# A convolution and a channel mix on one core: the start of the first pair in steps of 256 tokens, with its x loads on both sides of K's weights

## The chip, the core and the metric

One core of a Trainium2 chip runs the whole program in one launch. PE (TensorE) multiplies, ACT (ScalarE) and DVE (VectorE) work on tiles in SBUF and PSUM, POOL (GpSimd) and SP (SyncE) mostly issue DMAs. The metric is the device time of one execution in microseconds; the figure that counts is the median over runs. A profile is one execution recorded by the hardware.

## The reference

x is 8 x 4160 x 192 in float32. A causal convolution of 7 taps, one softmax-normalised set of taps for each of 8 heads of 24 channels, makes y. Then a channel mix with the token before:

```python
y  = causal_conv7(x, softmax(weight))            # per head
xk = mu_k * y + (1 - mu_k) * y_prev
xr = mu_r * y + (1 - mu_r) * y_prev
k  = maximum(xk @ w_k, 0)                        # 192 -> 1024
v  = (k * k) @ w_v                               # 1024 -> 192
out = sigmoid(xr @ w_r) * v
```

## The kernel before

The 8 sequences are worked on as 4 pairs; the two sequences of a pair lie in the two halves of the 128 partitions (64 channels of each), in three column blocks `c` of 64 channels. A pair is cut into **steps** of 512 tokens. The first pair has a first step of 256 and a last one of 256 (`sizes`, L62). K of a step is cut into **slots**: a slot is one PSUM tile of 1024 columns, two sequences of 512, that holds 128 rows of K for 512 tokens or 256 rows for 256 tokens, so a step of 256 has 4 slots and one of 512 has 8. Four slots make a **bundle**. `slots[2:8]` is put into another order (L73) so that bundle 0 needs only the first 512 columns of `w_k`.

For a slot, `k_mm` (L521) issues the matmuls into PSUM, `k_relu` (L545) is the ReLU on ACT, `k_square` (L551) squares on DVE. V's matmuls (`v_rows`, L615) follow some bundles later, R's (`r`, L586) in between. Before K, DVE makes `d = y - y_prev` (`diff`, L476), then `xk` and `xr` from it with a scale for each column block and one add (`scale` L505, `add_y` L515; `mix` calls both).

The convolution goes by **groups** of blocks of x (L88 to L98). For the first pair the groups 0, 1 and 2 (3, 4 and 4 blocks of 120 tokens) are convolved straight into the transposed layout by `conv_t` (L361), in which x is the stationary operand, and copied from PSUM to `yT` by `to_yT`. Group 3 goes through `conv_mm` (64x128 tiles of the array) and transposes on PE, groups from 4 on through `conv_tiles` (64x64 tiles), a buffer in DRAM and a transposing DMA (`y_write`, `y_read`).

The program is recorded in a fixed order: each engine's queue is the order in which the functions are called. `prologue` (L756) issues the loads and makes the masks and the band matrix `toe`. `bundle_first`, `bundle_second` and `bundle_third` are written out by hand; tables (`mix_a`, `mix_b`, `mix_c`, `late`) hold DVE work that is put into a bundle at given places, `rest` bundles follow one pattern. All loads of x and of the weights go through POOL's queue, in the order of the calls: x of group 1, first half of `w_k` (two DMAs, one for each half of the partitions), x of group 2, second half of `w_k`, x of group 3, `w_r`, `w_v`, x of group 4. The DMAs share eight semaphores in turn, so the ninth waits for the first to land. x of group 0 comes through the queues of ACT and SP.

PSUM is a ring of four tiles of two banks. A write into one bank of a tile waits for the reads of earlier data of this tile, of its other bank too, where the program has such a wait.

Of the kernel before, what the change touches and what calls it, by code (L numbers as in the profile page):

```python
# [14 lines left out]
def kernel(  # L15
# [43 lines left out]
    slots = []  # L59
    first_step = {}  # L60
    for p in range(NPAIR):
        sizes = [STEP // 2] + [STEP] * (S // STEP - 1) + [STEP // 2] if p == 0 else [STEP] * (S // STEP)  # L62
        t0 = 0
        first_step[p] = len(steps)
        if p == NPAIR - 1:
            sizes.append(NPAIR * TAIL)
        for L in sizes:
            ns = L * NF // STEP
            steps.append((p, t0, L, len(slots), ns))
            slots += [(len(steps) - 1, j) for j in range(ns)]  # L70
            t0 += L
    T0, LAST = S - TAIL, len(steps) - 1
    slots[2:8] = slots[4:8] + slots[2:4]  # L73
    NSLOT = len(slots)


# [21 lines left out]
        assert S <= base <= NROW  # L98


    xbs = {}

    def x_tile(g):
        p, base, nb, _, on_pe = groups[g]
        xb = three.tile([P, GB, 2, D], BF16, tag="xb", name="xb")
        xbs[g] = xb
        if g > 4:

            nc.vector.memset(xb[0:1, 0, 0, 0:2], 0.0)  # L109
        if base == 0:  # L110
            nc.gpsimd.memset(xb[0:32, 0, :, :], 0.0)  # L111
        if not on_pe and base + 2 * nb * HB > S:
            n0 = nb - (base + 2 * nb * HB - S) // HB - 1
            nc.gpsimd.memset(xb[Q:P, n0:nb, :, :], 0.0)

    def load_x(g):
        p, base, nb, _, on_pe = groups[g]
# [105 lines left out]
    def softmax():  # L223
        nc.vector.tensor_reduce(out=w_max, in_=w_raw, axis=mybir.AxisListType.X, op=ALU.max, negate=True)
        nc.scalar.activation(out=w_exp, in_=w_raw, func=AF.Exp, bias=w_max, accum_out=w_sum)
        nc.scalar.preload_act_table(AF.Sigmoid)
        xbs[0] = three.tile([P, GB, 2, D], BF16, tag="xb", name="xb")
        for c in range(NC):
            cs = slice(c * Q, (c + 1) * Q)
            nc.scalar.copy(out=xbs[0][:, : groups[0][2], :, cs], in_=x_f32[:, :, :, cs])  # L230
        nc.vector.reciprocal(out=w_sum, in_=w_sum)
        nc.vector.tensor_scalar(
            out=w_nrm[0:H, 0:K], in0=w_exp, scalar1=w_sum, scalar2=None, op0=ALU.mult
        )
        nc.vector.transpose(out=w_tap, in_=w_nrm)
        for r in range(8):
            nc.tensor.matmul(
                out=w_per[:, :, r], lhsT=tap8[:, 8 - r : 8 - r + P], rhs=w_tap[0:8, 0:H], start=True, stop=True
            )
# [265 lines left out]
    def scale(s, i, *cs):  # L505
        L = steps[s][2]
        if s not in (xks, xrs)[i]:
            (xks, xrs)[i][s] = two.tile([P, NC, STEP], BF16, tag=("xk", "xr")[i], name=("xk", "xr")[i])
        t = (xks, xrs)[i][s]
        for c in cs:  # L510
            nc.vector.tensor_scalar(  # L511
                out=t[:, c, :L], in0=diffs[s][:, c, :L], scalar1=mu[:, i, c : c + 1], scalar2=None, op0=ALU.mult
            )
# [194 lines left out]
    for s, (p, t0, L, n0, ns) in enumerate(steps):  # L708
        fb = first_bundle[s]
        if s == 0:  # L710
            at(mix_a, 1, mix, s, 1)
            continue
        if s == 1:
            at(mix_b, 1, scale, s, 1, 0, 1)
            at(late, 2, scale, s, 1, 2)
            at(late, 2, add_y, s, 1)
        else:
            if s == 2:
                at(mix_c, 1, diff, s)
            elif s == 4:  # L720
                at(mix_b, fb - 1, diff, s)
            else:
                at(mix_c, fb - 2, diff, s)
            at(mix_b if s == 4 else mix_a, fb - 1, scale, s, 0, 0)
            at(mix_b, fb - 1, scale, s, 0, 1, 2)
            at(mix_c, fb - 1, add_y, s, 0)
            if s == 2:
                at(mix_a, fb, scale, s, 1, 0)
                at(mix_b, fb, scale, s, 1, 1)
            else:  # L730
                at(mix_c, fb - 1, scale, s, 1, 0)
                at(mix_a, fb, scale, s, 1, 1)
            at(mix_b, fb, scale, s, 1, 2)
            at(mix_b, fb, add_y, s, 1)
        if s == LAST - 1 or s < LAST and steps[s + 1][0] > p:
            at(late, fb - 1, keep_tail, p)
    for s, j, vb in quads:
        b = vb - (s == LAST)
        if 0 < s < LAST - 1:
            b = min(b, first_bundle[s + 2] - 2 + j)  # L740
        at(rq, b, r, s, j)
        at(rs, b, r_out, s, j)
        if s == LAST:
            at(late, vb, v_last, s, j)
        else:
            vq.setdefault(vb, []).append((s, j))
# [9 lines left out]
    def prologue():  # L756
        nc.sync.dma_start(
            out=w_raw,
            in_=weight,
        )  # L760
        nc.vector.memset(x_f32[0:32, 0, :, :], 0.0)
        nc.vector.memset(ones_t, 1.0)
        for st, eng in ((0, nc.scalar), (1, nc.sync)):
            load_x_first(eng, 0, P, 1, groups[0][2], st, st + 1)
        load_x_first(nc.scalar, 16, P, 0, 1, 0, 2)
        load_x_first(nc.sync, HALO, 16, 0, 1, 0, 2)
        load_mu(0, moe_mu_k)
        load_mu(1, moe_mu_r)
        nc.scalar.preload_act_table(AF.Exp)
        nc.vector.memset(zeros, 0.0)  # L770
        nc.vector.memset(w_nrm, 0.0)
        nc.vector.memset(ones6, 1.0)
        x_tile(1)
        load_x(1)
        masks_tap()
        select_equal(ident6, 2 * NC)
        masks_band()
        load_wk(0, DF // 2)

        for i in range(SHORT):  # L780
            q = slice(i % 4 * 32, i % 4 * 32 + 32)
            nc.tensor.matmul(
                out=warm_ps[q, 0, 0:1], lhsT=ones_t[:, 0:32], rhs=ones_t[:, 0:1], start=True, stop=True
            )
        warm(warm_ps, WARM[0])
        x_tile(2)
        softmax()
        warm(warm_ps, WARM[1])
        make_toe()
        load_x(2)  # L790
        load_wk(DF // 2, DF)
        select_equal(ident, P)
        x_tile(3)
        load_x(3)
        load_wr()
        load_wv()
        x_tile(4)
        load_x(4)

    def bundle_first(ns):  # L800
        new_yT(0)
        tiles = [ring.tile([P, 2, BANK], FP32, tag="k", name="ps_t") for _ in range(2)]
        for n, (g, c) in enumerate((g, c) for g in range(2) for c in range(NC)):
            o = tiles[n % 2][:, n // 2 % 2, :]
            conv_t(g, c, o, range(groups[g][2]))
            if n == 0:
                turn_mu()
            to_yT(g, c, o, 0, groups[g][2], nc.scalar.copy)
            if g == 0:
                diff(0, slice(c, c + 1))  # L810
                if c == 0:
                    nc.vector.tensor_copy(out=mu.rearrange("p i c -> p (i c)"), in_=warm_ps[:, 1, 0 : 2 * NC])
                mix(0, 0, slice(c, c + 1))

        diff(1, slice(0, 1))
        mix(1, 0, slice(0, 1))
        for n in ns[:2]:
            k_mm(n)
            k_relu(n)
        diff(1, slice(1, 3))  # L820
        scale(1, 0, 1, 2)
        add_y(1, 0, slice(1, 3))
        for n in ns[2:]:
            k_mm(n)
            k_relu(n)
        for n in ns:
            k_square(n)
        run(late, 0)

    def bundle_second(b, ns):  # L830

        act_, dve_ = nc.scalar.copy, nc.vector.tensor_copy
        g = 2
        k_mm(ns[0])
        k_relu(ns[0])
        k_mm(ns[1])
        tiles = [ring.tile([P, 2, BANK], FP32, tag="k", name="ps_t") for _ in range(2)]
        outs = [tiles[0][:, 0, :], tiles[1][:, 0, :], tiles[0][:, 1, :]]
        conv_t(g, 0, outs[0], range(4))
        to_yT(g, 0, outs[0], 0, 4, dve_)  # L840
        k_relu(ns[1])
        conv_t(g, 1, outs[1], range(4))
        to_yT(g, 1, outs[1], 0, 4, dve_)
        k_mm(ns[2])
        k_relu(ns[2])
        conv_t(g, 2, outs[2], range(4))
        to_yT(g, 2, outs[2], 0, 4, act_)
        k_mm(ns[3])
        k_square(ns[0])
        run(mix_a, b)  # L850
        conv_half(xt[b][0], 0)
        k_relu(ns[3])
        conv_half(xt[b][0], 1)
        k_square(ns[1])
        run(mix_b, b)
        conv_mm(*xt[b][1], 0)
        conv_mm(*xt[b][1], 1)
        run(mix_c, b)
        run(late, b)
# [133 lines left out]
```

## Time and profile before

| | us |
|---|---|
| median of 3 runs (lowest, highest) | 413.19 (413.01, 413.28) |
| span of the profiled execution | 412.2 |
| PE busy | 403.7 (98%) |
| DVE busy | 370.5 (90%) |
| ACT busy | 353.2 (86%) |
| POOL busy | 64.1 (16%) |

The span runs from the first to the last instruction of the program. The time of a run is 0.99 us longer than the span of the profiled execution. Busy time of an engine is the union of its instructions; matmuls are pipelined, and a single one is listed with its whole latency, so that a sum of durations is more than the busy time. Where a row of the timeline merges several instructions, its length is that of the whole group. Rows name tiles as out<-in. `ps_t` is PSUM of `conv_t`, `ps_k` of K, `ps_c` of the other convolutions, `ps_v` of V, `ps_r` of R; `k_sb` is K after the ReLU, `k` its square.

The total by part of the chain that ended last, as shares of the span:

```profile
PE 88%; DMA 4%; DVE 3%; ACT 2%; issue 1%; POOL 1%; SPq 0%; POOLq 0%
```

### The profile page before, as it was taken

To read this page: it belongs to the slowest core of one execution; us is meant where nothing else is said; L and a number is where in the kernel's file an instruction comes from. 1 tells how busy PE (TensorE), PEld (TensorE's weight loads), DVE (VectorE), ACT (ScalarE), POOL (GpSimd) and SP (SyncE) were. 2 spreads that over 40 slices of the span, in tenths; PEclk is the share of its full clock that TensorE was granted. 3 is DMA by queue.
4 is the path that set the end of the run, shared out by engine and by line. 5 is a ranking of instruction groups with operands and counts; after the bars stand their busy time and mean duration, and the time that the engine had idled before them with its cause. 6 is when DMAs were issued, how large, how long until landed. Compare 5 with 4: busy or idle time off the path is not lost.

```text
span 412.2 us, 16799 instructions
## 1 busy us (share of the span) xinstructions
PE 403.7 (98%) x7349; PEld 301.7 (73%) x7350; DVE 370.5 (90%) x672; ACT 353.2 (86%) x426; POOL 64.1 (16%) x100
## 2 busy tenths in 40 slices
PE   7899999999999999999999999999999999999996
PEld 5567767767867777776777777777777777777795
DVE  5999799999999998999999999999989898999973
ACT  6899978889988888988888899888889888787781
POOL 8622023022040201104040110304000000000000
PEclk9999999999999999999999999999999999999999
DMA  9999989959978894998769697897863926321223
GB/s 141 192 200 194 191 200 190 253 133 194 198 110 211 151 214 118 200 218 113 198 121 229 156 196 182 111 226 130 188 163 100 184 82 175 107 67 53 80 80 115
DMA packets 137241, 65.58 MB, mean 159 GB/s; under 512 B 87356, under 2 KB 137168, under 8 KB 137168
## 3 DMA queue, kind: packets, MB, share of 16 engines
q1 hardware_dynamic: 95840, 48.42, 44.9%
q0 software_dynamic: 40528, 15.53, 33.0%
q8 instruction: 57, 0.93, 0.9%
q10 hardware_dynamic: 800, 0.57, 0.4%
q14 instruction: 16, 0.13, 0.1%
HBM read 31.62 MB, written 37.09 MB: 167 GB/s over the span
## 4 chain that ended last, share of the span: by engine, by line
PE 88%; DMA 4%; DVE 3%; ACT 2%; issue 1%; POOL 1%; SPq 0%; POOLq 0%
PE ps_v L625 39%; PE ps_k L537 37%; PE ps_r L594 7%; PE ps_c L302 3%; DMA yT<-y_dram 2%; DMA wk<-in_moe_w_k_dram 2%; DVE k L563 1%; PE ps_v L577 1%; DMA y_dram<-y 1%; ACT k_sb L549 1%; ACT y L319 0%; DVE d L480 0%; POOL xb L136 0%; DVE xr L511 0%; SPq L424 0%
## 5 line engine op out<-in xcount | busy, mean ns | idle before, releaser
L549 ACT ACTIVATE k_sb<-ps_k 128x1024 bf16<-128x1024 f32 x260 | 253.1, 1037 | 36.1 <-PE ps_k L537 35.2
L563 DVE TENSOR_TENSOR k<-k_sb 128x1024 bf16<-128x1024 bf16 x260 | 172.6, 685 | 28.3 <-ACT k_sb L549 27.9
L537 PE MATMUL ps_k<-xk,wk 64*128 64x512 bf16 (+1 forms) x1632 | 191.0, 367 | 1.2 <-DMA wk<-in_moe_w_k_dram 0.7
L625 PE MATMUL ps_v<-wv,k 64*128 64x192 bf16 x4032 | 188.2, 243 | 0.2 <-DVE k L563 0.2
L625 PEld LDWEIGHTS <-k 64*128 64x128 bf16 x4032 | 167.7, 94 | 13.6 <-issue 4.0
L537 PEld LDWEIGHTS <-wk 64*128 64x128 bf16 x1632 | 79.9, 94 | 59.6 <-DMA wk<-in_moe_w_k_dram 0.9
L136 POOL DMA_DIRECT2D xb<-in_x_dram x62 | 45.1, 738 | 171.2 <-issue 81.8
L641 DVE TENSOR_TENSOR o_sb<-ps_v,r_sb 128x768 f32<-128x768 f32 x64 | 60.8, 951 | 2.6 <-issue 2.4
L605 ACT ACTIVATE r_sb<-ps_r 128x768 bf16<-128x768 f32 x65 | 53.3, 821 | 10.6 <-PE ps_v L625 9.9
L319 ACT CAST y<-ps_c 128x960 bf16<-128x960 f32 (+5 forms) x84 | 50.7, 685 | 0.0
L594 PEld LDWEIGHTS <-xr 64*128 64x128 bf16 x780 | 34.5, 94 | 15.2 <-issue 1.0
L594 PE MATMUL ps_r<-wr,xr 64*128 64x192 bf16 x780 | 43.1, 243 | 0.5 <-DVE o_sb L641 0.5
L511 DVE TENSOR_SCALAR xr<-d,mu 128x512 bf16<-128x512 bf16 (+1 forms) x102 | 35.1, 348 | 0.0
L480 DVE TENSOR_TENSOR d<-yT 128x1536 bf16<-128x1536 bf16 (+4 forms) x36 | 31.3, 870 | 2.0 <-ACT yT L381 1.1
L511 DVE TENSOR_SCALAR xk<-d,mu 128x512 bf16<-128x512 bf16 (+1 forms) x99 | 32.0, 352 | 0.1
L517 DVE TENSOR_TENSOR xr<-xr,yT 128x1536 bf16<-128x1536 bf16 (+1 forms) x33 | 31.0, 938 | 1.1
L517 DVE TENSOR_TENSOR xk<-xk,yT 128x1536 bf16<-128x1536 bf16 (+3 forms) x33 | 30.4, 921 | 0.1
L302 PEld LDWEIGHTS <-toe 64*64 64x64 bf16 x448 | 9.6, 106 | 11.7 <-issue 10.7
L302 PE MATMUL ps_c<-xb,toe 64*64 64x240 bf16 (+1 forms) x448 | 16.6, 265 | 0.2 <-ACT k_sb L549 0.2
L464 POOL COPY y_tail<-yT 128x195 bf16<-128x195 bf16 x4 | 3.2, 796 | 64.9 <-DMA yT<-y_dram 64.8
L111 POOL MEMSET xb<- 32x384 bf16 x3 | 1.2, 407 | 45.2 <-DVE xb L109 39.2
L371 PEld LDWEIGHTS <-xb 128*32 128x32 bf16 (+3 forms) x264 | 5.3, 119 | 1.9 <-ACT xb L230 1.1
(57 smaller groups left out, 63.0 us busy)
## 6 DMA issues: line engine op xcount, KB each, us to landing
out_dram<-o_sb SPq DMA_DIRECT2D x128, 192.0 KB
xb<-in_x_dram POOLq DMA_DIRECT2D x40, 240.0 KB, 8.2
y_dram<-y SPq DMA_DIRECT2D x44, 210.0 KB
y_dram<-y SPq DMA_DIRECT2D x12, 168.0 KB
xb<-in_x_dram POOLq DMA_DIRECT2D x10, 192.0 KB, 5.5
xb<-in_x_dram POOLq DMA_DIRECT2D x6, 216.0 KB, 4.9
xb<-in_x_dram POOLq DMA_DIRECT2D x6, 144.0 KB, 5.3
wk<-in_moe_w_k_dram POOLq DMA_DIRECT2D x4, 192.0 KB, 7.1
```

The lines of the kernel that those rows point to most:

```text
L136: nc.gpsimd.dma_start(out=xb[q0 : q0 + rows, lo:hi, s, :], in_=bass.AP(tensor=x.tensor, offset=x.offset + (b * S + t0 + lo * step) * D, ap ...
L302: nc.tensor.matmul(out=banks[j * Q : (j + 1) * Q, i, :, :, k * G : (k + 1) * G], lhsT=toe[q, h, q], rhs=xbs[g][q, j * m : (j + 1) * m, :, ...
L319: nc.scalar.copy(out=bass.AP(tensor=y.tensor, offset=y.offset + d, ap=[y.ap[0], [m * 2 * D, 2], [2 * D, m], [Q, 2], [1, b - a]],), in_=bas ...
L511: nc.vector.tensor_scalar(out=t[:, c, :L], in0=diffs[s][:, c, :L], scalar1=mu[:, i, c : c + 1], scalar2=None, op0=ALU.mult)
L517: nc.vector.tensor_tensor(out=o, in0=o, in1=y_of(s, sl, 0), op=ALU.add)
L537: nc.tensor.matmul(out=ps[:, i, f * L : (f + 1) * L], lhsT=wk[r, c, fs], rhs=xk[r, c, :L], start=c == 0 and f == 0, stop=c == NC - 1 and f ...
L549: nc.scalar.activation(out=k_sb, in_=ps.rearrange("p a b -> p (a b)"), func=AF.Relu)
L563: nc.vector.tensor_tensor(out=o, in0=i, in1=i, op=ALU.mult)
L594: nc.tensor.matmul(out=ps[:, i, k * D : (k + 1) * D], lhsT=xr[q, c, ts], rhs=wr[q, c, :], start=c == 0, stop=c == NC - 1,)
L605: nc.scalar.activation(out=r_sbs[s, j], in_=r_ps.pop((s, j))[:, :, 0 : 2 * D], func=AF.Sigmoid)
L625: nc.tensor.matmul(out=v_ps[s, j][:, bank, k * D : (k + 1) * D], lhsT=k2s[s][q, f, t * P : (t + 1) * P], rhs=wv[q, f, :], start=half == 0 ...
L641: nc.vector.tensor_tensor(out=o_sb.rearrange("p (b t) d -> p b (t d)", b=2), in0=v_ps.pop((s, j)), in1=r_sbs.pop((s, j)), op=ALU.mult,)
```

## The change

The first pair's steps become 256, 256, 256, then 512 and so on: what was one second step of 512 tokens is two steps of 256. The order of slots in the first two bundles becomes: bundle 0 has the first two slots of steps 0 and 1, bundle 1 the last two of each, bundle 2 the four slots of step 2. The tables of DVE work are shifted to the new step numbers.

x of groups 1 and 2 now lies in one tile of eight blocks (`homes`). Its first two blocks are loaded ahead of the first half of `w_k`; then come both halves of `w_k`, and then the other six blocks in one DMA for each sequence. Bundle 0 convolves group 0 and two blocks of group 1; the other two blocks of group 1 are convolved in bundle 1, into one PSUM tile that one DVE copy of 3x240 columns empties. Group 2 is convolved after it; its first two column blocks go to the two banks of one PSUM tile, both copied by DVE, the third to another tile, copied by ACT.

```diff
-        sizes = [STEP // 2] + [STEP] * (S // STEP - 1) + [STEP // 2] if p == 0 else [STEP] * (S // STEP)
+        sizes = [STEP // 2] * 3 + [STEP] * (S // STEP - 2) + [STEP // 2] if p == 0 else [STEP] * (S // STEP)
...
-    slots[2:8] = slots[4:8] + slots[2:4]
+    slots[2:8] = slots[4:6] + slots[2:4] + slots[6:8]
...
+        home = homes[1][:, groups[1][2] :, :, :] if g == 2 else three.tile([P, GB, 2, D], BF16, tag="xb", name="xb")
+        homes[g] = home
+        xb = home[:, 0:nb, :, :]
...
+    def load_x_blocks(g, n0, n1):
+        base = groups[g][1]
+        for s in range(2):
+            nc.gpsimd.dma_start(
+                out=homes[g][:, n0:n1, s, :],
...
-            (xks, xrs)[i][s] = two.tile([P, NC, STEP], BF16, tag=("xk", "xr")[i], name=("xk", "xr")[i])
+            (xks, xrs)[i][s] = (two, three)[i].tile([P, NC, STEP], BF16, tag=("xk", "xr")[i], name=("xk", "xr")[i])
...
-        if s == 1:
-            at(mix_b, 1, scale, s, 1, 0, 1)
-            at(late, 2, scale, s, 1, 2)
-            at(late, 2, add_y, s, 1)
+        if s < 3:
+            at(mix_b, s + 1, mix, s, 1)
...
-        load_x(1)
+        load_x_blocks(1, 0, 2)
...
-        load_x(2)
         load_wk(DF // 2, DF)
+        load_x_blocks(1, 2, 4 + groups[2][2])
...
-            conv_t(g, c, o, range(groups[g][2]))
+            nb = (3, 2)[g]
+            conv_t(g, c, o, range(nb))
...
-        diff(1, slice(0, 1))
-        mix(1, 0, slice(0, 1))
-        for n in ns[:2]:
-            k_mm(n)
-            k_relu(n)
-        diff(1, slice(1, 3))
-        scale(1, 0, 1, 2)
-        add_y(1, 0, slice(1, 3))
-        for n in ns[2:]:
+        diff(1)
+        mix(1, 0)
+        for n in ns:
             k_mm(n)
             k_relu(n)
...
         k_mm(ns[1])
-        tiles = [ring.tile([P, 2, BANK], FP32, tag="k", name="ps_t") for _ in range(2)]
-        outs = [tiles[0][:, 0, :], tiles[1][:, 0, :], tiles[0][:, 1, :]]
-        conv_t(g, 0, outs[0], range(4))
-        to_yT(g, 0, outs[0], 0, 4, dve_)
+        t = ring.tile([P, 2, BANK], FP32, tag="k", name="ps_t").rearrange("p a (h t) -> p (a h) t", h=2)
+        for c in range(NC):
+            conv_t(1, c, t[:, c, :], (2, 3))
+        c0 = YC + groups[1][1] + 2 * BLK
+        nc.vector.tensor_copy(out=yTs[0][:, :, c0 : c0 + 2 * BLK], in_=t[:, 0:NC, 0 : 2 * BLK])
         k_relu(ns[1])
-        conv_t(g, 1, outs[1], range(4))
-        to_yT(g, 1, outs[1], 0, 4, dve_)
+        diff(2)
+        mix(2, 0)
         k_mm(ns[2])
         k_relu(ns[2])
-        conv_t(g, 2, outs[2], range(4))
-        to_yT(g, 2, outs[2], 0, 4, act_)
+        g = 2
+        tiles = [ring.tile([P, 2, BANK], FP32, tag="k", name="ps_t") for _ in range(2)]
+        for c in range(2):
+            conv_t(g, c, tiles[0][:, c, :], range(4))
+            to_yT(g, c, tiles[0][:, c, :], 0, 4, nc.vector.tensor_copy)
         k_mm(ns[3])
+        conv_t(g, 2, tiles[1][:, 0, :], range(4))
+        to_yT(g, 2, tiles[1][:, 0, :], 0, 4, nc.scalar.copy)
         k_square(ns[0])
```

In words, DVE's queue after the change reads, from the first difference of step 1 on: `d` and `xk` of step 1; the four squares of bundle 0; the copy of 3x240; `d` and `xk` of step 2; the two copies of group 2; a square; `xr` of step 0; a square; `d` of step 3 (tokens 768 to 1279); two squares; a scale of step 3's `xk`; two squares; `xr` of step 1; the other two scales and the add of step 3's `xk`. Bundle 3's matmuls are those of step 3.

## The prediction

> **What bounds the kernel now.** I read first the stretches by stage: how long each engine is busy in each part of the span. Columns: stretch, its length, then busy time and instructions of PE, PEld, DVE, ACT and POOL, granted clock, DMA share, GB/s.
>
> ```profile
> 16.00:22.30 6.30, 6.01 (x160) 4.44 (x157) 6.18 (x14) 6.13 (x9) 3.31 (x5) 1.00 1.59 190
> 22.30:28.00 5.70, 5.47 (x88) 3.67 (x87) 5.63 (x11) 5.05 (x8) 0.72 (x1) 1.00 1.60 191
> 28.00:38.00 10.00, 9.82 (x181) 7.13 (x181) 9.94 (x21) 9.66 (x14) 4.48 (x7) 1.00 1.32 185
> 62.20:400.00 337.80, 337.80 (x6064) 253.45 (x6062) 311.91 (x555) 296.20 (x352) 39.83 (x59) 1.00 0.75 156
> ```
>
> From 62 us on PE is never idle (337.80 of 337.80) and nothing of this change is there: what the change is worth is how much sooner or later the start hands over. From 16 to 38 the fullest engine is DVE (6.18 of 6.30, 5.63 of 5.70, 9.94 of 10.00), not PE. Next the start itself, in the timeline of the engines (start, length, instruction, count, idle time before it and what ended it):
>
> ```profile
> 11.42 1.70 PE L537 MATMUL ps_k<-xk,wk 64*128 64x256 bf16 x25 [0.71 <-DMA wk<-in_moe_w_k_dram]
> 12.28 6.63 ACT L549 ACTIVATE k_sb<-ps_k 128x1024 bf16<-128x1024 f32 x7 [1.18 <-PE ps_k L537]
> 13.34 0.69 DVE L563 TENSOR_TENSOR k<-k_sb 128x1024 bf16<-128x1024 bf16 x1
> 14.25 0.69 DVE L563 TENSOR_TENSOR k<-k_sb 128x1024 bf16<-128x1024 bf16 x1 [0.22 <-ACT k_sb L549]
> ...
> 16.70 1.21 DVE L381 CAST yT<-ps_t 128x480 bf16<-128x480 f32 x2
> ...
> 18.65 0.48 DVE L511 TENSOR_SCALAR xr<-d,mu 128x256 bf16<-128x256 bf16 x2
> 19.16 0.56 DVE L517 TENSOR_TENSOR xr<-xr,yT 128x768 bf16<-128x768 bf16 x1
> ...
> 20.24 0.84 DVE L511 TENSOR_SCALAR xr<-d,mu 128x512 bf16<-128x512 bf16 x2
> 21.00 0.94 DVE L480 TENSOR_TENSOR d<-yT 128x1536 bf16<-128x1536 bf16 x1
> ...
> 25.17 0.96 DVE L517 TENSOR_TENSOR xk<-xk,yT 128x1536 bf16<-128x1536 bf16 x1
> ```
>
> K's weights hold PE until 11.42; from there ACT's ReLUs pace the start (seven in 6.63, 0.95 each); from 16.1 DVE has no idle time to speak of. Its queue ends in the `xk` of tokens 768 to 1279 at 25.17 + 0.96 = 26.13, and PE opens bundle 3 on those tokens at 26.66, 0.5 later: that matmul is the handover I count to. The chain that ended last agrees (start, length, what):
>
> ```profile
> 4.84 6.53 DMA wk<-in_moe_w_k_dram
> ...
> 16.09 0.69 DVE k L563
> 16.78 0.29 DVE yT L381
> ...
> 22.47 0.69 DVE k L563
> 23.16 0.05 issue
> 23.20 1.00 PE ps_v L625 x20
> ```
>
> It runs through K's weights, then ReLU and DVE up to 23.2, then PE.
>
> **The change part by part.** All durations are of this one execution, 412.2 of span; the median of the runs is 413.19, so 0.99 lies around the span and is carried along. Each step's difference is added to 413.19.
>
> *Loads.* POOL issues two 128x2 blocks in place of two 128x4 ones (0.91 and 0.78 before), so K's first half goes out some 0.25 earlier. In the DMA queue half of 393 KB is gone ahead of it: at the 190 GB/s above 1.0 us. K's first half, landed at 4.84 + 6.53 = 11.37, should land near 9.9; bounds 11.1 (only the issue counts) and 9.6. Behind it K's second half (393 KB) and six x blocks (590 KB) take 983 / 190 = 5.2 us, so x would be whole at 15.1; the same eight transfers ended at 15.47 before. I take 15.3, with 16.5 (11.3 + 5.2) as the late end. The loads behind, of groups 3 and 4, `wr` and `wv`, keep their places; SP's queue is unchanged.
>
> *Convolution on PE.* Ahead of K go 48 matmuls less (two of the seven blocks). PE runs them at 100 ns per four at that point in the trace (144 in 3.86, waits in it), later 64 in 1.02. The three ACT copies shrink from 0.56 (480 columns) to about 0.36 for 240 (0.46 for 360). Each group-1 part waits for the copy two or three places before it, as now: copies end near 9.05, 9.6 and 10.15, so the difference for step 1 starts at 10.2.
>
> *Step 1 as 256 tokens.* The difference is 768 wide: 0.56, as the 128x768 add at 19.16. Three scales and the add took 18.45 to 19.64, 1.19 start to start. So `xk` of step 1 is ready at 10.2 + 0.5 + 1.25 = 11.95, against 13.36. That frees the first square: 13.34 becomes 11.95, **1.39 won**. The first two slots' ReLUs (from 10.8) are done by then.
>
> K's matmuls: twelve of 256 columns took 0.83, six of 512 took 0.81. The same per slot, and 0.02 lies under a ReLU of 1.02. Without that cover 16 slots would cost 0.3.
>
> *Work that DVE gains ahead of the handover.* One copy of 720 columns from PSUM: two of 480 took 1.21, so 0.6 each, 0.78 start to start for 720 (bounds 0.6 and 0.9). `xk` of tokens 512 to 767: 0.5 + 1.19 = 1.69. `xr` of step 1 in full (1.19) where before only two scales (0.84) stood there: 0.35. Together **2.82 more**. The ten squares, the two 480 copies, the first `xr` and the whole `xk` of tokens 768 to 1279 stand there in both.
>
> *Waits on DVE.* The third slot's K can only start with `xk` at 11.95; 0.85 of matmul and 1.02 of ReLU bring its square to 13.9, where DVE is free at 13.2: 0.7 idle. The fourth waits 0.3 (14.6 to 14.85). Then DVE is free at 15.5 and its next instruction is the new copy: x at 15.3, 48 matmuls and their latency, 0.9, so 16.2: 0.7 idle. One new wait is in the code: group 2's second column block goes to the other bank of the same PSUM tile as the first, and its matmul waits until the first's copy has left. That copy stands behind step 2's `xk`, at 18.7 to 19.25. Behind the waiting matmul on PE stand 32 of convolution, the last slot of bundle 1, the third block and group 3's convolution; ACT's copy and ReLU wait for those. DVE itself idles 0.6 (matmuls 19.3 to 19.85). In all 2.3, against 0.22 + 0.23 + 0.22 = 0.67 before: **1.6 more**.
>
> *Sum.* 26.13 + 2.82 - 1.39 + 1.6 = 29.2 for the `xk` that opens bundle 3, and PE starts there at 29.2 and not 26.66: +2.6. PE itself would be free at about 27 (last square of step 0 at 22.9, then 64 V matmuls and two slots in 4.1). In bundle 3 step 2's `xr` (1.19) is added to a DVE busy 9.94 of 10.00; V's matmuls there don't read it, so I take 0.2 of a possible 0.5. Total +2.8: 413.19 + 2.8 = **416.0**. PE's idle 0.76 between 50 and 62, behind the transposed read of y, moves along, since its whole chain starts in bundle 3.
>
> *A rule that speaks against it.* The trace's own row: the convolution's matmuls come four per 100 ns until 10.1 and four per 50 ns after, at a granted clock shown as 1.00. The Trainium skill, "TensorE: Matmul & The Clock Gate", Part 1, says that the array stays at half clock until a free-running window of about 3.4 us has been busy. By it a PE that idles before K's weights may stay slow for one more window; the third slot would then take 0.65 longer, and as the wait for x covers that, the sum would be the same 416.0, and up to 0.65 more where x is early.
>
> **The rivals.** (1) *x comes late.* For: the six blocks are now behind all of K's weights in one queue, at a DMA share of 1.5 to 1.6. If they are whole at 16.5 and not 15.3, the copy and all of DVE behind it move by 1.2: 417.2. Against: K's first half has less ahead of it. (2) *The waits close.* x lands by 14.4 and the bank wait falls under DVE's work: 0.7 and 0.6 of the 2.3 go, and with the bundle-3 term 1.5 in all: 414.5; with the copy at its lower bound 414.3. For: 1.6 of the 2.8 is waits, and those are the loosest numbers. (3) *Faster.* K's weights decide, as the chain of before says: the first ReLU moves from 12.28 to 10.85, 1.4, and the bundles follow: 411.8. It decides from the point where DVE's queue to the handover ends before 26.66 - 1.4 = 25.3, 3.9 sooner than my sum. Against: 2.82 of added work on an engine that has 0.1 idle in each 6 us there. (4) *Nothing moves.* The loads gain only 0.25 and the shorter steps give back what they cost: 413.2. Part of the description has no edit behind it anyway: the 64x128 convolution of group 3 stands as it was.
>
> **How the numbers follow.** The forecast 416.0 (415 to 416.8) gets 0.58, late x 0.15, closed waits 0.14, nothing 0.05, faster 0.08. Runs tell a change from none from about 0.2%, 0.83 us. So faster 0.08, same 0.05, slower 0.58 + 0.15 + 0.14 = 0.87. The range is 414.2 to 417.4: below, the closed waits; above, late x with the bundle-3 term at 0.2; it leaves out cases 3 and 4 and the edge of 1.
>
> **What would show it.** Right: first square near 12; first K weight wait shorter, K near 10; PE idle on DVE's yT copy (2 us and more) inside group 2's convolution; DVE without gaps from 16 to 29; PE idle 2 us before bundle 3 on `xk`; everything after shifted. Wrong: the `xk` of 768 columns ready after 13, a first square no sooner than 13.3 (loads gave nothing), or bundle 3 opening before 26.7 (then DVE was not the bound and case 3 holds).

## The result and the profile after

| | before | after |
|---|---|---|
| median (lowest, highest) | 413.24 (413.01, 413.40), 4 runs | 418.41 (417.71, 418.94), 4 runs |
| profiled execution: time, span | span 412.2 | 418.44, span 416.6 |
| first half of K's weights landed | 11.37 | 9.56 |
| first square on DVE | 13.34 | 11.90 |
| `xk` of tokens 768 to 1279 ready | 26.14 | 31.12 |
| bundle 3's first K matmul | 26.66 | 31.18 |
| V matmul number 193 / 321 | 43.80 / 56.77 | 49.08 / 61.18 |

The ratio is 1.0117, 95% interval 1.0092 to 1.0141: slower, by 5.2 us where 2.8 was forecast. The stretches of the changed kernel, in the same columns as before (stretch, its length, busy time and instructions of PE, PEld, DVE, ACT and POOL, granted clock, DMA share, GB/s):

```profile
16.00:22.30 6.30, 3.36 (x134) 2.54 (x134) 3.89 (x9) 1.70 (x2) 1.42 (x2) 1.00 1.59 191
22.30:28.00 5.70, 5.42 (x126) 4.74 (x126) 5.61 (x14) 4.98 (x7) 2.85 (x4) 1.00 1.51 176
...
66.60:404.00 337.40, 337.40 (x6055) 253.07 (x6053) 311.53 (x554) 296.01 (x352) 39.84 (x59) 1.00 0.76 157
```

Late in the program PE is again never idle, so all of the loss is in the start. There the stretch from 16.0 to 22.3 has lost its engines: DVE is busy 3.89 of 6.30 where it was 6.18, PE 3.36 where it was 6.01. The timeline of PE (start, length, instruction, count, idle time before it and what ended it) says where:

```profile
9.60 1.55 PE L550 MATMUL ps_k<-xk,wk 64*128 64x256 bf16 x24
12.04 2.79 PE L550 MATMUL ps_k<-xk,wk 64*128 64x256 bf16 x48 [0.89 <-DVE xk L530]
14.80 0.23 PE L384 MATMUL ps_t<-toe,xb 128*32 128x120 bf16 x2
16.75 0.81 PE L384 MATMUL ps_t<-toe,xb 128*32 128x120 bf16 x46 [1.72 <-DMA xb<-in_x_dram]
...
21.04 0.60 PE L384 MATMUL ps_t<-toe,xb 128*32 128x120 bf16 x32 [2.19 <-DVE yT L394]
...
31.18 1.47 PE L550 MATMUL ps_k<-xk,wk 64*128 64x512 bf16 x12 [0.75 <-DVE xk L530]
```

The row at 16.75 is the convolution of group 1's last two blocks, held by its load; the one at 21.04 is group 2's second column block, held by the copy of the first out of the other bank of its PSUM tile. DVE's timeline has the same two gaps, in front of the copy of 3x240 and of the second 480 copy:

```profile
11.90 1.30 DVE L576 TENSOR_TENSOR k<-k_sb 128x1024 bf16<-128x1024 bf16 x2
13.96 0.69 DVE L576 TENSOR_TENSOR k<-k_sb 128x1024 bf16<-128x1024 bf16 x1 [0.77 <-ACT k_sb L562]
...
17.60 0.91 DVE L846 CAST yT<-ps_t 128x720 bf16<-128x720 f32 x1 [2.03 <-PE ps_t L384]
...
21.69 0.66 DVE L394 CAST yT<-ps_t 128x480 bf16<-128x480 f32 x1 [0.70 <-PE ps_t L384]
```

After 21.69 DVE has no gap of note up to the add that ends at 31.12. The chain that ended last (start, length, what) now runs through x's transfer and not the weights', and goes on over DVE:

```profile
7.49 9.22 DMA xb<-in_x_dram
16.71 0.04 issue
16.75 0.83 PE ps_t L384 x24
17.58 0.02 issue
17.60 0.92 DVE yT L846
...
20.42 0.58 DVE yT L394
21.00 0.04 issue
21.04 0.60 PE ps_t L384 x32
...
30.16 0.97 DVE xk L530
31.14 0.04 issue
31.18 0.84 PE ps_k L550 x6
```

### The profile page after: what moved, and what is told of

It reads as the page before. It is cut to its first block, busy times and chain, and to the rows that moved or that the text cites. A ratio compares the mean times of both kernels' runs of the same rounds, so it can differ in the third digit from the quotient of the medians.

```text
span 416.6 us, 16900 instructions
## 1 busy us (share of the span) xinstructions
PE 404.0 (97%) x7398; PEld 303.4 (73%) x7398; DVE 371.8 (89%) x680; ACT 352.7 (85%) x426; POOL 64.2 (15%) x100
## 4 chain that ended last, share of the span: by engine, by line
PE 91%; DVE 3%; DMA 2%; POOL 1%; ACT 1%; issue 1%; POOLq 0%; ACTq 0%
PE ps_v L638 40%; PE ps_k L550 38%; PE ps_r L607 8%; PE ps_c L315 3%; DMA xb<-in_x_dram 2%; PE ps_v L590 1%; DVE k L576 1%; ACT k_sb L562 1%; POOL wk L222 1%; POOL xb L121 1%; PE ps_t L384 0%; DVE xk L530 0%; DVE xk L524 0%; DVE d L493 0%; DVE yT L846 0%
## 5 line engine op out<-in xcount | busy, mean ns | idle before, releaser
L550 PEld LDWEIGHTS <-wk 64*128 64x128 bf16 x1680 | 82.2, 94 | 58.6 <-DVE xk L530 2.1
L150 POOL DMA_DIRECT2D xb<-in_x_dram x58 | 41.8, 730 | 174.7 <-issue 81.8
L493 DVE TENSOR_TENSOR d<-yT 128x1536 bf16<-128x1536 bf16 (+2 forms) x36 | 31.3, 870 | 1.5 <-ACT yT L394 1.4
L530 DVE TENSOR_TENSOR xk<-xk,yT 128x1536 bf16<-128x1536 bf16 (+1 forms) x33 | 30.4, 921 | 0.1
L384 PE MATMUL ps_t<-toe,xb 128*32 128x120 bf16 (+3 forms) x264 | 6.6, 256 | 4.1 <-DVE yT L394 2.2
```

The costliest lines, as they stand in the source:

```text
L150: nc.gpsimd.dma_start(out=xb[q0 : q0 + rows, lo:hi, s, :], in_=bass.AP(tensor=x.tensor, offset=x.offset + (b * S + t0 + lo * step) * D, ap ...
L530: nc.vector.tensor_tensor(out=o, in0=o, in1=y_of(s, sl, 0), op=ALU.add)
L550: nc.tensor.matmul(out=ps[:, i, f * L : (f + 1) * L], lhsT=wk[r, c, fs], rhs=xk[r, c, :L], start=c == 0 and f == 0, stop=c == NC - 1 and f ...
```

## The experiments

The kernel before, run beside each set, had medians of 413.8 to 414.0. Unless a diff says otherwise it is against the changed kernel.

**Is it the load? (a1_split_x)** The six blocks behind the weights, in one DMA for each sequence, are cut into the two that are convolved first and the four of group 2.

```diff
-        load_x_blocks(1, 2, 4 + groups[2][2])
+        load_x_blocks(1, 2, 4)
+        load_x_blocks(1, 4, 4 + groups[2][2])
```

> The changed kernel, with its six late x blocks loaded as two (the rest of group 1) and then four (group 2). Theory A: the x wait of 1.72 us in front of the 3x240 copy is a cost of its own and DVE's queue behind that copy moves with it; the two blocks land near 14.4, the copy starts at 15.6 and not 17.60, bundle 3's first K at 29.2 and not 31.18: 416.4. Rival B: the bank wait of 2.19 us on PE decides, x does not: 418.2 to 418.6. Rival C: the loss lies outside the start (clock, time around the span): 418.4.

Measured 417.38 (416.04 to 418.15), ratio 1.0072 [1.0045, 1.0099]. The two blocks landed at 13.75 and the copy started at 15.28, 2.3 sooner than in the changed kernel; the wait for x was gone. But bundle 3 opened at 30.23, only 0.95 sooner. The time between went into something neither theory had. Two stretches of this kernel show it in the clock column, behind the five engines:

```profile
18.70:21.30 2.60, 2.58 (x56) 1.74 (x59) 1.25 (x2) 0.00 (x0) 0.00 (x0) 0.50 1.60 192
21.30:22.80 1.50, 1.41 (x44) 1.06 (x33) 0.72 (x5) 0.77 (x2) 0.39 (x1) 0.83 1.60 191
```

and so do the rows of PE in its timeline:

```profile
18.72 0.99 PE L384 MATMUL ps_t<-toe,xb 128*32 128x120 bf16 x32 [2.20 <-DVE yT L394]
19.65 1.46 PE L550 MATMUL ps_k<-xk,wk 64*128 64x256 bf16 x12
21.04 0.94 PE L384 MATMUL ps_t<-toe,xb 128*32 128x120 bf16 x32
```

and those of DVE in the same stretch:

```profile
19.76 0.66 DVE L394 CAST yT<-ps_t 128x480 bf16<-128x480 f32 x1 [1.09 <-PE ps_t L384]
20.34 0.68 DVE L576 TENSOR_TENSOR k<-k_sb 128x1024 bf16<-128x1024 bf16 x1
22.04 0.28 DVE L524 TENSOR_SCALAR xr<-d,mu 128x256 bf16<-128x256 bf16 x1 [1.03 <-issue]
```

After 2.20 us without work PE runs at a granted clock of 0.50: 32 matmuls take 0.99 and not 0.60, twelve of K 1.46 and not 0.83. DVE waits 1.09 (0.70 at full clock) and then 1.03 more. That second wait is put down to nothing in the profile; next to it in DVE's queue stands a write into `xb`, which PE's convolution read until 21.98, so this is taken as its cause. Together DVE loses 1.42 by the clock. The one run of a1 with a mean clock of 1.000 over its span took 416.04; the three at 0.994 to 0.996 took 417.33 to 418.15. So the theory of the late load holds in the one run in which the clock stays up (416.4 was expected), and hides behind the clock in the others.

**Is it the bank? (a2_two_tiles)** The first two column blocks of group 2 go to two PSUM tiles, as before the change.

```diff
-            conv_t(g, c, tiles[0][:, c, :], range(4))
-            to_yT(g, c, tiles[0][:, c, :], 0, 4, nc.vector.tensor_copy)
+            conv_t(g, c, tiles[c][:, 0, :], range(4))
+            to_yT(g, c, tiles[c][:, 0, :], 0, 4, nc.vector.tensor_copy)
...
-        conv_t(g, 2, tiles[1][:, 0, :], range(4))
-        to_yT(g, 2, tiles[1][:, 0, :], 0, 4, nc.scalar.copy)
+        conv_t(g, 2, tiles[0][:, 1, :], range(4))
+        to_yT(g, 2, tiles[0][:, 1, :], 0, 4, nc.scalar.copy)
```

> The changed kernel, with group 2's column blocks 0 and 1 in two PSUM tiles, so that the second one's matmuls no longer wait for the copy of the first. Theory A (DVE's queue decides): only DVE's idle time of 0.70 before the second copy goes: 417.7. Rival B (PE's wait of 2.19 decides): about 2 us go: 416.3. The x wait stays in both.

Measured 417.42 (416.81 to 417.58), ratio 1.0071 [1.0047, 1.0095]. DVE's two copies stand together, x was late as ever (whole at 16.81), and bundle 3 opened at 30.36, 0.82 sooner. DVE's timeline:

```profile
17.70 0.91 DVE L846 CAST yT<-ps_t 128x720 bf16<-128x720 f32 x1 [1.76 <-PE ps_t L384]
...
20.43 1.22 DVE L394 CAST yT<-ps_t 128x480 bf16<-128x480 f32 x2
```

This is the smaller value: the bank wait costs DVE its 0.7 and little more while the clock stays up.

**Is it work in DVE's queue? (a3_xr_after)** `xr` of step 1, ahead of the add that opens bundle 3, is moved behind it.

```diff
-            at(mix_b, s + 1, mix, s, 1)
+            at((mix_b, late, mix_b)[s], s + 1, mix, s, 1)
```

> The changed kernel, with xr of step 1 (three scales and an add, 1.2 us of DVE) moved behind xk of tokens 768 to 1279 in DVE's queue; the same work is done. Theory A (DVE's queue up to that xk is what PE waits for): bundle 3's first K at 30.0 and not 31.18, and 417.2 if DVE has room later. Rival: DVE has no room before 38 us and the work is paid in bundle 3: 418.2 to 418.6.

Measured 418.35 (417.02 to 418.91), ratio 1.0094 [1.0068, 1.0120]. The median can't tell it from the changed kernel. In the profiled execution (417.02, the lowest of the four) the add ended at 29.30, 1.82 sooner, of which 0.65 was x (whole at 16.06 there); 0.3 was then lost, since bundle 3 opened at 29.61 when PE was free. The three runs with a mean clock of 0.994 to 0.996 took 418.35 and more. Inconclusive in time, in favour of the theory in the timeline.

**Why is x late? (b1_weights_first, a6_weights_issued_sooner)** One is the kernel before with the two halves of K's weights back to back, ahead of x of group 2:

```diff
-        load_x(2)
         load_wk(DF // 2, DF)
+        load_x(2)
```

> The kernel of before, with only the order of two loads changed: the second half of w_k ahead of x of group 2. Theory A (four weight transfers one behind the other leave the DMA engines underused, so that the same eight transfers end later): the last of the eight lands at 16.5 to 16.9 where it was 15.47, group 2's convolution starts at 16.7 and not 15.89, time 413.8 to 414.3. Rival: the order does not change the total, last landing 15.3 to 15.6, convolution at 15.9, time 413.2.

Measured 414.39 (413.47 to 415.97), ratio 1.0010 [0.9994, 1.0026]. The last of the eight transfers landed at 15.79, 15.47 before. The order by itself is not what made the six blocks land at 16.71. Next, the last two columns (DMA share, GB/s) of the stretch right behind the first x, in the kernel before:

```profile
5.00:6.50 1.50, 1.35 (x27) 0.59 (x25) 1.09 (x4) 1.34 (x3) 1.50 (x3) 1.00 1.42 172
```

and in the changed one:

```profile
5.00:6.50 1.50, 1.31 (x27) 0.55 (x25) 1.10 (x4) 1.31 (x3) 1.50 (x3) 1.00 0.93 76
```

With half of x ahead the queue moves 76 GB/s where it moved 172, before the weights' packets come: (172 - 76) x 1.5 us = 144 KB, or 0.76 us at 190 GB/s. So the first half of the weights was issued sooner, ahead of the masks' first part on POOL:

```diff
         load_x_blocks(1, 0, 2)
+        load_wk(0, DF // 2)
         masks_tap()
         select_equal(ident6, 2 * NC)
         masks_band()
-        load_wk(0, DF // 2)
```

> The changed kernel, with the first half of w_k issued by POOL ahead of the masks (1.1 us sooner); the masks, the band matrix and so the convolution come 1.2 later. Asked of it: why x is whole only at 16.7. Theory A (with half the x ahead the DMA queue runs empty before the weights' packets arrive, 76 GB/s from 5.0 to 6.5 against 172 before): the hole closes, over 130 GB/s in that stretch, and the last of the eight loads lands at 15.6 to 16.1. Rival (weight packets back to back are slow by themselves): 16.6 or later. Time 417.4 to 418.4, since the chain through the convolution is 1.2 later.

Measured 418.02 (417.32 to 419.21), ratio 1.0097 [1.0072, 1.0123]. The hole filled only in part (111 GB/s) and the six blocks were whole at 16.22, between the two expectations. In the kernels that keep the six blocks in one DMA for each sequence x was whole anywhere from 16.06 to 16.81, in those that split it between 15.78 and 16.09. The hole by itself doesn't explain this: a1 has it too (61 GB/s in the same stretch) and had all of x at 15.79. What holds the unsplit load beyond 15.8 stays open. In this profiled execution the clock dropped too, as its stretches show:

```profile
18.70:20.50 1.80, 0.00 (x0) 0.00 (x0) 1.76 (x5) 0.19 (x1) 0.00 (x0) 1.00 1.62 199
20.50:24.00 3.50, 3.46 (x80) 2.37 (x80) 1.35 (x4) 0.10 (x1) 0.00 (x0) 0.51 1.59 187
```

**The load undone (a5_four_ahead)** All four blocks of group 1 are loaded ahead of the weights, as before; steps and convolution stay changed.

```diff
-        load_x_blocks(1, 0, 2)
+        load_x_blocks(1, 0, 4)
...
-        load_x_blocks(1, 2, 4 + groups[2][2])
+        load_x_blocks(1, 4, 4 + groups[2][2])
```

> The changed kernel, with four x blocks ahead of K's weights as before, then all of w_k, then the four of group 2: the steps of 256 stay, the loads' halving goes. Theory A (the early K is worth nothing, since DVE's added work is what the start waits for): first K back at 11.4 to 11.8, no x wait in bundle 1, the 3x240 copy at 17.0, bundle 3's first K at 30.4 to 30.8, time 417.5 to 418.1. Rival (K's earlier start is a gain that the x wait hides): 1.5 later than the changed kernel, 419.5 or more.

Measured 419.04 (418.49 to 419.83), ratio 1.0123 [1.0098, 1.0148]. The first square was back at 13.27 and x was not waited for in bundle 1, so the copy came at 16.63, 0.97 sooner than in the changed kernel (17.0 was expected). The bank wait was 2.53, and the half clock followed, by the mean clock in all four runs (0.994 to 0.996), which the theory did not have; bundle 3 opened at 31.64, not at 30.4 to 30.8. The row of PE:

```profile
20.09 0.99 PE L384 MATMUL ps_t<-toe,xb 128*32 128x120 bf16 x32 [2.53 <-DVE yT L394]
```

Without the load's part the change is no faster. Held against the two runs of the changed kernel with the same mean clock (418.38 and 418.94), these four (418.49 to 419.83) are level or a little slower: the head start and the late x about cancel.

**Three parts mended at once (a4_split_tiles_xr)** The edits of a1, a2 and a3 together.

> The changed kernel with all three edits together: late x split in two and four blocks, group 2's first two column blocks in two PSUM tiles, xr of step 1 behind xk of tokens 768 to 1279. Theory A (each shortens DVE's queue before bundle 3; in the run with x alone the PE wait of 2.20 that was left was followed by matmuls at half speed, 0.99 for 32 of the convolution and 1.46 for 12 of K, which here goes with the wait): bundle 3's first K at 26.9 to 27.4 and the time 413.9 to 414.5. Rival (the three gains overlap, or PE at half speed comes from the x wait and not the bank wait): first K of bundle 3 at 28.5 or later, 415.5 or more.

Measured 415.29 (414.46 to 417.67), ratio 1.0039 [1.0018, 1.0059]. The profiled execution (414.99) opened bundle 3 at 27.40. DVE's timeline, behind its last square of bundle 0 that ends at 15.8:

```profile
15.84 0.91 DVE L847 CAST yT<-ps_t 128x720 bf16<-128x720 f32 x1
16.78 0.56 DVE L493 TENSOR_TENSOR d<-yT 128x768 bf16<-128x768 bf16 x1
```

and the one wait that PE has left in group 2's convolution:

```profile
19.36 0.60 PE L384 MATMUL ps_t<-toe,xb 128*32 128x120 bf16 x32 [1.03 <-DVE yT L394]
```

DVE has no gap from its fourth square to beyond the add, and the add still ends 1.20 later than before: 27.34 against 26.14. From the first square to there it takes 14.96, before 12.80: this is the work that the smaller step brings, with next to no wait. PE opened bundle 3 right behind it, without a wait of its own. The third column block still waits 1.03 for a bank; of ten runs, two had a mean clock of 0.994 and 0.996 and took 417.6 and 417.7, the other eight 414.5 to 416.7; no profile shows where those two lost it.

**Is the half clock PE's idle time? (a7_filler)** a1 with matmuls that nothing reads, put on PE just ahead of the convolution that waits for the bank.

```diff
         for c in range(2):
+            if c == 1:
+                warm(tiles[1], 8)
             conv_t(g, c, tiles[0][:, c, :], range(4))
```

> The a1 kernel (x split behind the weights) with eight filler matmuls of 512 columns, into a PSUM tile that is written over afterwards, put on PE just ahead of the convolution that waited 2.2 us for a PSUM bank. What is computed stays as it is. Theory (the half clock in a1 comes from PE's 2.2 us without work): PE has no wait above 1 us there, the granted clock stays at full speed through 18.7 to 21.3 us, the convolution's 32 matmuls take 0.60 us (0.99 in a1) and K's twelve 0.83 (1.46), DVE idles at most 0.9 us at its c1 copy (1.09 in a1), xk's add ends some 1.2 to 1.5 sooner, bundle 3 opens at 28.7 to 29.1, and the time is 415.8 to 416.3. Rival (the speed follows something else, a phase of the execution that a filler doesn't touch): half speed again at the same place, bundle 3 at about 30.2, time 417.4. Second rival (the fillers delay the bank's own convolution): DVE idles longer than 1.1 us and the time is 417.4 or more.

Measured 416.44 (416.08 to 416.80), ratio 1.0056 [1.0044, 1.0068]; all six runs had a mean clock of 0.999 or 1.000. The same two stretches as in a1:

```profile
18.70:21.30 2.60, 2.24 (x82) 1.64 (x81) 1.84 (x5) 0.07 (x1) 0.00 (x0) 1.00 1.60 193
21.30:22.80 1.50, 1.28 (x22) 0.92 (x20) 1.47 (x6) 1.50 (x3) 1.19 (x2) 1.00 1.59 190
```

and the rows of PE, the first of which is the filler (seven of its eight are in the trace):

```profile
17.02 1.90 PE L765 MATMUL ps_t<-zeros,ones_t 128*128 128x512 bf16 x7
19.28 0.60 PE L384 MATMUL ps_t<-toe,xb 128*32 128x120 bf16 x32 [0.36 <-DVE yT L394]
19.82 0.83 PE L550 MATMUL ps_k<-xk,wk 64*128 64x256 bf16 x12
```

DVE's wait at the second copy was 0.70 again. Bundle 3 opened at 29.43, later than the 29.1 expected, because the first square came at 12.35 and not 11.55; from first square to bundle 3 it took 17.08, in a1 18.68: 1.60 less. Of that 0.24 lies ahead of the copy of 3x240, where the filler does nothing; from the copy on it is 13.59 against 14.95, 1.36 less. With work on PE in the gap the drop is gone in six of six runs, without it a1 has it in three of four: PE's idle time decides, and not a phase of the execution that PE's work can't touch.

**Can the new order win? (a8_best, b2_xr_after)** a8 is a4 with more taken off DVE: two copies by ACT, `xr` of step 0 behind a copy.

```diff
-            at(mix_a, 1, mix, s, 1)
...
-        nc.vector.tensor_copy(out=yTs[0][:, :, c0 : c0 + 2 * BLK], in_=t[:, 0:NC, 0 : 2 * BLK])
+        nc.scalar.copy(out=yTs[0][:, :, c0 : c0 + 2 * BLK], in_=t[:, 0:NC, 0 : 2 * BLK])
...
+        mix(0, 1)
...
-            to_yT(g, c, tiles[c][:, 0, :], 0, 4, nc.vector.tensor_copy)
+            to_yT(g, c, tiles[c][:, 0, :], 0, 4, (nc.vector.tensor_copy, nc.scalar.copy)[c])
```

> The a4 kernel (x split, two tiles, xr later) with the two copies that PE's convolution and K wait for on ScalarE instead of VectorE (the 3x240 copy at the head and the copy of c1), and the residual's x of the first step moved behind the copy of c0. What is computed stays as it is. Theory (what was left of the loss in a4, 0.7 us at bundle 3, is VectorE's own queue): the chain of VectorE loses 0.9 and 0.6 us of copies and ends some 0.9 to 1.5 sooner, bundle 3 opens at 25.9 to 26.5 (26.66 before, 27.40 in a4), and the time is 412.5 to 413.7, level with the kernel before or just under it. Rival (ScalarE's copies come later than VectorE's did, because ScalarE has squares and roots of its own in its queue): bundle 3 opens at 27.2 or later, time 415 or more.

Measured 415.24 (414.30 to 415.93), ratio 1.0028 [1.0016, 1.0040]. In the profiled execution, the lowest of its eight, the `xk` that opens bundle 3 was ready at 26.30, 1.04 sooner than in a4 and 0.16 later than in the kernel before. But bundle 3 opened at 27.14, 0.48 after the old kernel. The rows:

```profile
19.07 0.60 PE L384 MATMUL ps_t<-toe,xb 128*32 128x120 bf16 x32 [1.07 <-DVE yT L394]
25.34 0.96 DVE L530 TENSOR_TENSOR xk<-xk,yT 128x1536 bf16<-128x1536 bf16 x1
27.14 1.47 PE L550 MATMUL ps_k<-xk,wk 64*128 64x512 bf16 x12
...
38.12 0.67 PE L607 MATMUL ps_r<-wr,xr 64*128 64x192 bf16 x12 [0.53 <-DVE o_sb L654]
```

The row at 27.14 has no wait: `xk` had been there for 0.84, and PE was still busy with what stands ahead in its own queue (7.82 of 8.07 us from 19.07 on, where the third column block had waited 1.07 for its bank). So the theory was right about DVE, and with DVE relieved PE's queue sets the handover. The time is the rival's, but not for its reason: ACT's two copies began at 15.39 and 17.85, both sooner than DVE's in a4. Behind it another 0.71 went: V matmul 129 came at 38.62, 37.43 before, after a late `o_sb` on DVE. From bundle 3 to that matmul the changed kernel takes 0.75 more than the kernel before and a4, with `xr` of step 1 pushed past the handover, 1.21: what is pushed past it is not free there. b2 is the kernel before with two scales of `xr` moved past the handover:

```diff
-            at(mix_b, 1, scale, s, 1, 0, 1)
-            at(late, 2, scale, s, 1, 2)
+            at(late, 2, scale, s, 1, 0, 1, 2)
```

> The kernel of before, with all three scales of step 1's xr behind the xk of tokens 768 to 1279 (two of them, 0.84 us of DVE, stood ahead of it). Theory A (DVE's queue paces 16 to 26 us there too): that xk ends 25.3 and not 26.14, V of step 0 starts 0.5 sooner, bundle 3's first K at 26.0 to 26.3, time 0.3 to 0.6 less than before. Rival: DVE is full up to 38 us and pays it in bundle 3: within 0.2 of before.

Measured 413.64 (413.35 to 414.57), ratio 0.9996 [0.9984, 1.0008]; in the profile bundle 3 opened 0.69 sooner, of which 0.34 was there at the first square already. No version was found that is faster than the kernel before by more than the runs can tell.

## Why the prediction was wrong, step by step

The direction and the waits that were named held; the size was 2.4 short, and a drop of the clock came on top in some runs. The table goes by the profiled executions (its terms sum to 2.5; the forecast rounded 0.07 up). That of the changed kernel (mean clock 0.999) has no drop of the clock in the start, so none of the terms is the half clock:

| step | predicted | measured | share of the 2.4 |
|---|---|---|---|
| first square | 11.95 | 11.90 | 0 |
| third and fourth square wait | 0.7, 0.3 | 0.77, 0.22 | 0 |
| x whole, so the copy of 3x240 starts | 15.3, 16.2 | 16.71, 17.60 | +1.40 |
| from that copy to the add's end | 13.0 | 13.52 | +0.52 |
| from the add to bundle 3's first K | 0 | 0.06 | +0.06 |
| from bundle 3's first K to V matmul 321 | +0.2 | -0.11 | -0.31 |
| around the span | 0.99 | 1.84 | +0.85 |

- *Head start: right.* The 1.39 came as 1.44, with K's first half landed at 9.56 and not 9.9.
- *"Loads", "I take 15.3": the step that failed most.* It was taken near the 15.47 of the old transfers although the bound on the other side, 16.5, was written beside it. That bound was passed (16.71; 16.06 and 16.81 in a3 and a2, which load x in the same way), so the first rival's event took place; the second (the waits close), third (the weights decide) and fourth (nothing moves) fell with a copy at 17.60 and bundle 3 at 31.18. The sum let the queue run at 190 GB/s; the trace has 76 in one stretch and 140 to 163 in the four behind it, up to 12.5 us.
- *Waits: one right, one short.* The bank wait was 0.70 of DVE, 0.6 forecast, and 2.19 of PE. The wait for x was 2.03, 0.7 forecast. The price of all waits was 3.72 - 0.67 = 3.05, not 1.6.
- *DVE's work: small errors of one sign.* The copy of 720 columns takes 0.95 start to start, at 0.78 taken, and `d` and `xk` of step 2 take 1.79 at 1.69. Between the copy and the bank wait that is 0.27 of the 0.52; 0.1 is the bank wait, and the rest is not followed further.
- *Bundle 3 and behind: right in sum by two errors.* Up to V matmul 193 it lost 0.75 more (0.2 forecast, "of a possible 0.5"), with PE's 0.57 wait for `o_sb`; up to matmul 321 it gained 0.87, since the idle time behind the transposed read of y, which was to move along, was gone. (The 0.76 that the prediction gives for it is a gap of the weight loads; PE itself idled 0.54 there.)
- *Around the span: mis-sized.* The 0.99 set the median beside another execution's span. All executions with both figures have 1.65 to 1.84 between time and span, so the profiled execution of before, whose own time is not known, was some 0.7 to 0.85 longer than the median.
- *PE idle 2 us before bundle 3: wrong.* It was 0.75, since PE, held by x and the bank, was itself late. The DVE queue still set the handover here; in a8, with DVE relieved, PE's queue did, at 27.14, near the "about 27" of the prediction.
- *The rule of the clock: placed wrongly.* It was weighed at K's start only. The changed kernel's own profile has no drop there or at the bank wait (granted clock 1.00 in all stretches shown), but two of its four runs have a mean clock of 0.995 and 0.996, the value of the executions of a1, a5 and a6 whose profiles show the drop. The drop's price, about 1.4, is shown by a1 against a7. How much of the changed kernel's median it is was not tried by itself; its two runs without the drop took 417.71 and 418.44, the two with it 418.38 and 418.94, so that most of the 2.4 is there without it.

What the change costs is then: x late 1.4 to 2, the bank wait 0.7 (a2: 0.82 at bundle 3), the added work of DVE, of which 0.7 at bundle 3 is left when those two waits are gone and one `xr` is moved behind (a4; with more taken off DVE 0.5 is left, behind PE's own queue, a8), and the half clock in some executions.

## What to carry to other kernels

Before a load is cut to free a queue for what stands behind it, price the far end of what is put off, at the slowest rate that the trace has around there, and see who waits for its last byte: here a head start of 1.4 went back at the same engine 5 us later. A wait that looks cheap because the bound engine loses only 0.7 by it can be dear for another: 2.2 us without work on PE cost about 1.4 more here when the clock dropped, and work that nothing reads, put into the gap, kept it up. To compare a sum with a median, take the time around the span from an execution that has both.

## What the hardware showed that was not expected

- The granted clock fell to half after PE's waits of 2.20 (a1), 2.53 (a5) and 2.18 us (a6), and stayed there for 3.4 us each time: from the clock shares of half-microsecond stretches, 18.38 to 21.80, 20.09 to 23.51 and 20.53 to 23.95. The Trainium skill, "TensorE: Matmul & The Clock Gate", Part 1, gives a free-running window of 3413 ns, which fits this length, and has the array go cold after an idle window of about 3.4 us; here gaps of some 2.2 us sufficed, with PE busy in about 1.6, 0.9 and 1.2 of the 3.42 us ahead of the drop.
- The same gap did not drop it every time: 2.19 in the profiles of the changed kernel and of a3 went by at 1.00. The traces suggest that it depends on where the gap falls. Each of these profiles has a drop behind the last matmul too. In a1, a5 and a6 it comes at 414.33, 416.04 and 416.48, each time 395.95 us behind the first drop, which is 116 times 3.413: both stand on one grid of that step. Counted back from the last drop of the changed kernel (415.96) and of a3 (414.57), the gap is shared by two stretches of the grid in the first, with PE busy 2.10 and 2.28 of 3.41, and lies mostly in one in the second, with 1.64. The stretches ahead of the drops in a1, a5 and a6 have 1.55, 0.88 and 1.24. So the least work that kept the clock up lies between 1.55 and 1.64 us of a stretch, an estimate from these five executions.
- The mean clock of a run tells whether it had such a drop, since one stretch is 0.5 x 3.42 / 416 = 0.004 of it, and the means fall in two groups, 0.994 to 0.996 and 0.998 to 1.000. By that the drop was in two of four runs of the changed kernel and of a6, three of four of a1 and a3, four of four of a5, two of ten of a4, one of ten of b1, one of the 45 of the kernel before that were run beside them, and none of a2, a7, a8 and b2. Where it fell in a4, b1 and the kernel before no profile shows.
